# A state-space layer with a dense network on one core: K permuted and transposed by DMA, table G loaded without its zeros

## The chip, the core and the metric

The kernel runs on one core of a Trainium2 chip. A core has a matrix engine (PE; its weight loads are listed apart as PEld), a vector engine (DVE), a scalar engine (ACT), a general engine (POOL) and a queue engine (SP) that issues most transfers. Each takes its own instructions strictly in order. The metric is the time of one execution in microseconds (us). Before the change the median of 3 runs is 222.39 us (221.74 to 222.77).

## What is computed

```python
x = A_q                                               # 2048 x 640, bf16
k_shift = sum over t of k_pad[:, t:t+S] * shift_k[:, 3-t]   # 4 taps along the sequence
kv = k_shift * v
y  = causal long convolution of kv with ssm_k (by FFT), bf16
y  = y + kv * ssm_D
h  = x + layernorm(x) * y
h2 = h + Mish(layernorm(h) @ w1 + b1) @ w2            # 640 -> 1728 -> 640
```

S is 2048 and D is 640, batch 1. All inputs and the output are bf16.

## The kernel before

The sequence position is split as 16 times t1 plus t2: a partition holds t1 (128), and 16 rows t2 lie in it. Channels are taken in five blocks m of 128. The long convolution is a Fourier transform in two steps, a product, and the inverse in two steps, all as matmuls with tables.

The steps, by the names that the order list uses (pe is the matmul, ev the copy of its result out of PSUM to SBUF):

- k1 (L635): transposes of the long filter ssm_k; s1k (L561, L562) its first transform step, s2k (L662) its second, with table G as weights. Results lie in tile uk. One s2k unit is three matmuls of 160 columns and one copy of 480 columns; s2k needs all copies of s1k.
- kt (L590): per block m, 16 matmul transposes of K into kt_s; ktev copies them out of PSUM (1024 bf16 columns at a time, 10 copies); ktsh (L601, POOL) writes a third plane, shifted by one position.
- wsh (L516, POOL): weights for the 4-tap filter from the coefficients (coef, computed by cfpe from shift_k) and a 16-wide mask.
- kspe (L609, L610): the 4-tap filter as matmuls of kt_s with wsh; kv (L613, DVE) multiplies by V while leaving PSUM.
- s1v (L561, L562) and s2v (L697): the two transform steps of kv, with G as weights; results in uv.
- sw (L678, L679, SP): copies uk with even and odd partitions swapped; p1 and p2 (L716, L720; DVE or POOL): the products.
- i1 (L756, L757) and i2 (L813): the inverse steps; y copies the result out of PSUM.
- ln1, lnx, wb, h, bn, hc: the two layer norms; trd (L849) transposes the normalized rows by DMA, trpe by matmul for the first two.
- m1 (L910, L890) with Mish on ACT (L915), m2 (L943, L931), res (L948), d_out.

ORDER, a list written into the kernel, gives each step its engine (t PE, v DVE, a ACT, p POOL, d SP's queue, s ACT's queue) and its place on that engine. `unit` makes a pair of matmul and copy, as halves x and y. Copies out of PSUM are done by ACT (L428) or DVE (L430). PSUM has 8 banks, handed out by the same order.

Channels are read as `(d m l)`, so that a block m takes every fifth group of four channels, and 128 elements of K (8 positions by 16 channels) lie at one step of 40. G is 128 blocks of 128 x 128, 32 KB a partition, and three quarters of it are zeros: a row for channel offset dl (row modulo 4) has values only in columns of the same offset.

SP's queue loads, in this order: ssm_k blocks 0, 2, 3; x (four tiles); ssm_k 1, 4; K in four parts; G in eight parts of 512 KB with V in two parts among them; then the swaps.

## Time and profile before

| | |
|---|---|
| median of 3 runs | 222.39 us |
| span of the profiled execution (first to last instruction) | 219.6 us |
| granted PE clock | 1.00 throughout |
| PE busy | 212.6 us |
| DVE busy | 145.1 us |
| ACT busy | 133.1 us |
| POOL busy | 75.6 us |
| moved by DMA | 31.03 MB |

The span of the profiled execution is 2.8 us below the median of the runs; the time around the span (start and end of the program) is in the runs only. In the rows of the profile L561 is line 561 of the kernel, `out<-in` names the tiles, and "idle before, releaser" says how long the engine waited ahead of such instructions and what ended the wait. Rows of the chain that ended last show start, duration, and the work; rows in order of time show start, duration, engine, line and count.

### The profile page before, as it was taken

To read this page: it belongs to the slowest core of one execution; us is meant where nothing else is said; L and a number is where in the kernel's file an instruction comes from. 1 tells how busy PE (TensorE), PEld (TensorE's weight loads), DVE (VectorE), ACT (ScalarE), POOL (GpSimd) and SP (SyncE) were. 2 spreads that over 40 slices of the span, in tenths; PEclk is the share of its full clock that TensorE was granted. 3 is DMA by queue.
4 is the path that set the end of the run, shared out by engine and by line. 5 is a ranking of instruction groups with operands and counts; after the bars stand their busy time and mean duration, and the time that the engine had idled before them with its cause. 6 is when DMAs were issued, how large, how long until landed. Compare 5 with 4: busy or idle time off the path is not lost.

```text
span 219.6 us, 6285 instructions
## 1 busy us (share of the span) xinstructions
PE 212.6 (97%) x2611; PEld 157.8 (72%) x2618; DVE 145.1 (66%) x324; ACT 133.1 (61%) x265; POOL 75.6 (34%) x112
## 2 busy tenths in 40 slices
PE   8999999999989999999999999999999999999993
PEld 2899889999879999899876644566554444656672
DVE  0799999999999999989699889883210000213023
ACT  2488899999999999997881178600036475300000
POOL 0079997089844007124883371411000000000000
PEclk9999999999999999999999999999999999999999
DMA  6999993417999906996004401552720000000113
GB/s 213 375 419 414 412 403 130 98 23 174 192 263 285 380 10 217 325 359 105 0 0 64 91 14 45 50 103 60 86 79 19 0 3 0 0 0 3 54 60 125
DMA packets 32876, 31.03 MB, mean 141 GB/s; under 512 B 19024, under 2 KB 29264, under 8 KB 32464
## 3 DMA queue, kind: packets, MB, share of 16 engines
q1 hardware_dynamic: 32384, 30.43, 46.3%
q8 instruction: 20, 0.33, 0.7%
q10 hardware_dynamic: 368, 0.20, 0.4%
q14 instruction: 8, 0.07, 0.1%
q0 software_dynamic: 96, 0.00, 0.0%
HBM read 20.47 MB, written 2.62 MB: 105 GB/s over the span
## 4 chain that ended last, share of the span: by engine, by line
PE 76%; ACT 11%; DVE 5%; issue 3%; SPq 2%; DMA 1%; DVEq 0%; ACTq 0%
PE ps L943 26%; PE ps L910 26%; ACT uk L428 8%; PE ps L813 4%; ACT uv L428 3%; PE ps L756 3%; PE ps L757 3%; PE ps L635 2%; PE ps L561 2%; PE ps L473 2%; PE ps L590 2%; DMA xa<-uk 1%; DVE ra L613 1%; PE ps L931 1%; DVE uv L716 1%
## 5 line engine op out<-in xcount | busy, mean ns | idle before, releaser
L910 PE MATMUL ps<-G 128*128 128x512 bf16 (+1 forms) x319 | 58.5, 336 | 0.3
L943 PE MATMUL ps<-rn,uv 128*128 128x320 bf16 (+2 forms) x415 | 58.5, 299 | 0.1
L915 ACT ACTIVATE uv<-ps,b1s 128x512 bf16<-128x512 f32 (+1 forms) x65 | 35.6, 607 | 36.6 <-PE ps L910 34.8
L943 PEld LDWEIGHTS <-uv 128*128 128x128 bf16 x416 | 39.2, 98 | 18.5 <-issue 1.6
L910 PEld LDWEIGHTS <-G 128*128 128x128 bf16 x325 | 31.1, 98 | 24.0 <-issue 0.9
L428 ACT CAST uk<-ps 128x512 bf16<-128x512 f32 (+1 forms) x91 | 47.2, 703 | 1.9 <-PE ps L562 1.4
L948 DVE TENSOR_TENSOR xb<-ps,xb 128x320 bf16<-128x320 f32 (+2 forms) x12 | 5.6, 488 | 42.6 <-ACT uv L915 24.3
L428 ACT CAST uv<-ps 128x512 bf16<-128x512 f32 (+2 forms) x54 | 28.6, 766 | 0.0
L430 DVE CAST uk<-ps 128x512 bf16<-128x512 f32 (+2 forms) x32 | 20.1, 661 | 0.6 <-ACT uk L428 0.5
L756 PE MATMUL ps<-a,uv 128*128 128x128 bf16 x160 | 18.7, 219 | 0.4 <-DVE uv L716 0.3
L756 PEld LDWEIGHTS <-uv 128*128 128x128 bf16 x160 | 17.8, 114 | 0.9 <-DVE uv L716 0.5
L837 POOL TENSOR_TENSOR r<-ve,mhalf 128x1 f32<-128x1 f32 x16 | 9.7, 613 | 25.0 <-DVE ve L834 24.9
L430 DVE CAST uv<-ps 128x512 bf16<-128x512 f32 (+2 forms) x28 | 17.2, 669 | 0.2 <-ACT uv L428 0.2
L948 DVE TENSOR_TENSOR xa<-ps,xa 128x320 bf16<-128x320 f32 x12 | 5.6, 486 | 14.0 <-PE ps L943 13.9
L613 DVE TENSOR_TENSOR ra<-ps,rb 128x512 bf16<-128x512 f32 x20 | 12.9, 683 | 0.3 <-ACT uv L428 0.3
L720 POOL TENSOR_TENSOR rn<-rn,uv 128x1024 bf16<-128x1024 bf16 x5 | 10.6, 2127 | 7.2 <-PE ps L697 7.2
L697 PE MATMUL ps<-uv,G 128*128 128x64 bf16 (+1 forms) x256 | 12.2, 197 | 0.8 <-ACT uv L428 0.6
L662 PE MATMUL ps<-uk,G 128*128 128x160 bf16 x128 | 12.4, 230 | 0.3 <-ACT uk L428 0.2
L697 PEld LDWEIGHTS <-G 128*128 128x128 bf16 x256 | 10.8, 96 | 1.4 <-issue 1.0
L428 ACT CAST rb<-ps 128x512 bf16<-128x512 f32 (+1 forms) x30 | 11.3, 464 | 0.7 <-PE ps L813 0.4
L561 PE MATMUL ps<-cst,ra 128*64 128x128 bf16 x160 | 10.7, 219 | 0.4
L562 PE MATMUL ps<-cst,ra 128*64 128x128 bf16 x160 | 10.9, 222 | 0.0
(111 smaller groups left out, 375.7 us busy)
## 6 DMA issues: line engine op xcount, KB each, us to landing
G<-tab_g SPq DMA_DIRECT2D x8, 512.0 KB, 14.1
rn<-in_A_ssm_k_dram SPq DMA_DIRECT2D x5, 512.0 KB, 6.3
ra<-in_A_k_dram SPq DMA_DIRECT2D x4, 640.0 KB, 11.4
rb<-in_A_v_dram SPq DMA_DIRECT2D x2, 1280.0 KB, 13.9
G<-in_B_w_dram SPq DMA_DIRECT2D x5, 432.0 KB, 7.3
rn<-in_B_w_dram SPq DMA_DIRECT2D x1, 2080.0 KB, 13.4
rn<-uk SPq DMA_DIRECT2D x8, 256.0 KB, 4.3
rb<-uk SPq DMA_DIRECT2D x8, 256.0 KB, 4.5
```

The costliest lines, as they stand in the source:

```text
L428: nc.scalar.copy(o, i)
L430: nc.vector.tensor_copy(o, i)
L561: nc.tensor.matmul(ps[0:64, k, :], lhs, mc, start=True, stop=True)
L562: nc.tensor.matmul(ps[64:128, k, :], lhs, ms, start=True, stop=True)
L613: nc.vector.tensor_tensor(kv_w[:, m, k:32:2, 8 * h:8 * h + 8, :], ps.rearrange("p (l t d) -> p d t l", l=4, t=8), raw_v[:, 8 * h:8 * h + 8 ...
L662: nc.tensor.matmul(ps[:, o:o + 160], g_v[:, f, :], KA[:, :, f, :], start=True, stop=True)
L697: nc.tensor.matmul(ps[:, fl * n:fl * n + n], g_v[:, f0 + h * kf + fl, :], VX[x][:, :, f0 + h * kf + fl, :], start=True, stop=True)
L756: nc.tensor.matmul(pz[:, k, :], V[c.i][:, dg // 4, :, dg % 4], a12[:, 0, :], start=True, stop=False)
L910: nc.tensor.matmul(ph[:, 0:w], w1[:, dc, fc * P:fc * P + P], lnhT_of(u)[:, dc, 0:w], start=(dc == 0), stop=(dc == NDC - 1))
L915: nc.scalar.activation(hb_of(u)[:, fc, 0:w], rt.tile[:, 0:w], ACT.Mish, bias=b1s[:, fc:fc + 1], scale=1.0)
L943: nc.tensor.matmul(po[:, 0:d1 - d0], hb_of(u)[:, fc, tl * P:(tl + 1) * P], w2[:, fc, d0:d1], start=False, stop=(fc == NFC - 2))
L948: nc.vector.tensor_tensor(x, rt.tile[:, 0:d1 - d0], x, ALU.add)
```

## The change

Channels are now read as `(m p)`, contiguous blocks of 128. K is no longer transposed by PE: a copy kp (10 of 1024 columns; POOL nine, ACT one) permutes it within SBUF into buffers KP, and a DMA transpose kx on SP's queue writes kt_s, whose planes now lie in one row of 272 so that the shifted plane is a slice of it. ktpe, ktev and ktsh are gone.

```diff
-                nc.tensor.transpose(ps[:, q, :], raw_k[:, h * 8 * D + r:(h + 1) * 8 * D:40], ident)
...
-            ev(e, kt_s[b][:, :, h, :], ps.bitcast(BF16).rearrange("p (q t) -> p q t", q=8))
...
-            nc.gpsimd.tensor_copy(t[:, :, 2, 1:128], t[:, :, 1, 0:127])
...
+                src = raw_k[:, h * 8 * D:(h + 1) * 8 * D].rearrange("p (t c) -> p t c", t=8)[:, :, m * P:(m + 1) * P].rearrange("p t (q j) -> p q t j", j=16)
+                out = KP[m, h].rearrange("p (q t j) -> p q t j", q=8, t=8)
+                if e == "act":
+                    nc.scalar.copy(out, src)
+                else:
+                    (nc.vector if e == "dve" else nc.gpsimd).tensor_copy(out, src)
+            kps[m, h] = OP(f"kp{m}_{h}", [("pool", 1.3), ("dve", 0.55), ("act", 0.95)], d_k[2 * h:2 * h + 2], emit=kpf)
+
+            def kxf(e, m=m, h=h):
+                nc.sync.dma_start_transpose(kt_s[m][:, :, 144 - 128 * h:272 - 128 * h], KP[m, h])
+            kxs[m, h] = OP(f"kx{m}_{h}", ("dma", 1.5), [kps[m, h]], emit=kxf, lat=2.6)
```

KP lies in xb, in the hc tile and in the part of rn that held ssm_k blocks 2 to 4, so kp4_1 and the five kp of h = 0 wait for the k1 transposes of those blocks, and the swaps into rn wait for the kx.

```diff
+    KP = {(m, 1): x for m, x in enumerate([xb[:, 0:1024], xb[:, 1024:2048], xb[:, 2048:3072], hc_t[:, 0:1024], rn[:, 2 * S:2 * S + 1024]])}
+    KP |= {(m, 0): rn[:, 2 * S + 1024 * (m + 1):2 * S + 1024 * (m + 2)] for m in range(NDC)}
...
+    for i, k in enumerate([(4, 1)] + [(m, 0) for m in range(NDC)]):
+        kps[k].deps += k1_by[2 + i // 2]
```

G is stored without its zeros (1 MB) and loaded by eight transfers of 32 partitions by 16 pieces of 256 bytes; four memsets of 4096 columns (gz) write zeros first, one on DVE and three on POOL. Within a group of four blocks the columns are interleaved, so that a weight load now reads with a step of four elements. Each half of G needs four of the loads, and s2k and s2v wait for a half.

```diff
-    g_v = gt[:].rearrange("p (f q) -> p f q", q=P)
+    g_v = gt[:].rearrange("p (b q f) -> p b f q", q=P, f=4)
...
-        return lambda: nc.sync.dma_start(gt[:, i * 2048:(i + 1) * 2048], dram["g"][:, i * 2048:(i + 1) * 2048])
+        d, h = i % 4, i // 4
+        return lambda: nc.sync.dma_start(gt[d:P:4, h * 8192:h * 8192 + 8192].rearrange("p (b q) -> p b q", q=512)[:, :, 128 * d:128 * d + 128], dram["g"][d, :, h * 2048:h * 2048 + 2048].rearrange("p (b q) -> p b q", q=128))
+    c_gz = [OP(f"gz{i}", [("dve", 2.2), ("pool", 4.2)], emit=(lambda e, i=i: (nc.vector if e == "dve" else nc.gpsimd).memset(gt[:, i * 4096:(i + 1) * 4096], 0.0))) for i in range(4)]
...
-    d_g = [DMA(f"d_g{i}", 0.525e6, emit_g(i), deps=d_n[:1], prio=0.6, lat=4.9) for i in range(8)]
+    d_g = [DMA(f"d_g{i}", 0.131e6, emit_g(i), deps=d_n[:1] + c_gz[i // 4 * 2:i // 4 * 2 + 2], prio=0.6, lat=3.5) for i in range(8)]
```

Smaller edits follow from the new channel order: shift_k is loaded in pieces of 4 elements (8 bytes), ssm_D by five rows and one matmul instead of four, the coefficients are written four times over (1760 columns instead of 440), the mask has 176 columns, kv and y write contiguous runs.

```diff
-    d_sk = OP("d_sk", ("dmaS", 0.5), [d_row1], emit=lambda e: nc.scalar.dma_start(sk_r[:], A_shift_k.rearrange("(d n) j -> d (n j)", n=40)), lat=5.0)
+    d_sk = OP("d_sk", ("dmaS", 0.5), [d_row1], emit=lambda e: nc.scalar.dma_start(sk_r[:].rearrange("p (n j) -> p n j", j=4), A_shift_k.rearrange("(n d) j -> d n j", d=16)), lat=5.0)
...
-        ev(e, coef[:], cf_rt.tile[:, 0:440])
+        ev(e, coef[:].rearrange("p (r l) -> p r l", l=4), cf_rt.tile[:, 0:440].unsqueeze(2).to_broadcast([P, 440, 4]))
```

ORDER is written anew. Up to the first i2 matmul ACT has 4 k1, 26 s1k, 29 s2k, 28 s1v, 32 s2v and 33 i1 copies and one kp (before 3, 25, 32, 24, 30, 33 and 4 ktev); DVE has 6 k1, 14 s1k, 14 s2k, 12 s1v, 10 s2v, 5 i1 copies, 20 kv, 30 products and one memset (before 7, 15, 11, 16, 12, 4, 20, 27 and 6 ktev). Of the lnx 9 run on POOL instead of 7, and ACT has 29 y copies instead of 30. PE does all of s1k ahead of s2k, and 26 s2k units ahead of the first kspe. The new orders of POOL and of SP's queue:

```
POOL: gz1 gz3 kz gz0 wsh1_1 wsh1_0 wsh0_0 kp1_0 kp0_0 kp4_0 ln1p1 wsh0_1 kp0_1 kp2_1 kp1_1 kp2_0 wsh4_0 wsh2_0 kp3_1 wsh3_0 kp4_1 wsh3_1 wsh2_1 wsh4_1 p2_0_1 p2_0_3 d_small p1_0_0 p1_0_2 ...
SP:   d_n0 d_n2 d_x0 d_n1 d_n3 d_n4 d_g6 d_g7 d_k1 d_g5 d_k0 d_g4 d_g2 d_k3 d_k2 d_g1 d_g0 d_g3 d_v1 kx0_0 d_v0 kx0_1 kx1_0 kx1_1 kx3_0 kx2_0 kx2_1 kx3_1 kx4_0 kx4_1 sw0_0 sw0_1 sw0_3 sw0_2 sw1_0 sw2_1 ...
ACT:  warm k1ev0y k1ev2y s1kev0_2x s1kev0_1x s1kev2_3y s1kev0_2y s1kev0_3y s1kev2_2x coef ... kp3_0 (after the last s1kev) s2kev_20y ...
```

## The prediction

> **What bounds the kernel now.** I read the busy time by stretches first, because shares over the whole span mix stages. The columns are the stretch, its length, then busy time of PE, PEld, DVE, ACT and POOL, the granted clock, the DMA share and GB/s.

> ```profile
> core 0: us, PE busy (x) PEld busy (x) DVE busy (x) ACT busy (x) POOL busy (x), PEclk, DMA share, GB/s
> 0.00:8.30 8.30, 7.32 (x51) 3.92 (x53) 2.01 (x8) 1.49 (x2) 0.52 (x10) 1.00 0.79 261
> 8.30:34.00 25.70, 25.14 (x552) 23.56 (x553) 24.69 (x50) 23.06 (x41) 21.23 (x24) 1.00 1.02 410
> 34.00:87.00 53.00, 51.20 (x1093) 48.36 (x1092) 52.09 (x86) 53.00 (x112) 26.27 (x24) 1.00 0.62 169
> 87.00:96.00 9.00, 9.00 (x97) 7.84 (x95) 8.70 (x23) 8.78 (x24) 1.74 (x3) 1.00 0.97 344
> 96.00:216.00 120.00, 119.63 (x828) 73.98 (x834) 57.23 (x161) 46.77 (x89) 25.88 (x53) 1.00 0.24 49
> ```

> The last row is the dense network (m1, m2): PE works 119.63 of 120 us, and the change takes nothing from its matmuls. Whatever the change is worth, it is by how much earlier that block starts. Ahead of it, from 34 to 87 us, ACT has no idle time at all and DVE 0.9 us: the copies out of PSUM set the pace. PE looks as busy, but a busy PE in this view is not a full one.

> The waits of ACT up to 90 us are the next view (who waited for whom: total, times, longest), then two rows in order of time that show where each of the two engines starts.

> ```profile
> ACT rb L428 <- PE ps L635: 5.2, 1, 5.2
> ACT uk L428 <- PE ps L562: 1.4, 2, 0.7
> ACT uv L428 <- PE ps L590: 0.7, 1, 0.7
> ACT uk L428 <- PE ps L662: 0.5, 1, 0.5
> 6.73 0.69 DVE L430 COPY xa<-ps 128x1024 bf16<-128x1024 bf16 x1 [0.28 <-PE ps L635]
> 8.31 1.01 ACT L428 COPY rb<-ps 128x1024 bf16<-128x1024 bf16 x1 [5.20 <-PE ps L635]
> ```

> ACT begins copying at 8.31 us, 1.6 us after DVE, and later waits for PE for 1.4 + 0.7 + 0.5 = 2.6 us, before 34 us, while PE also transposes K (L590). After that it never waits. So the front can end sooner in two ways: less copying for ACT and DVE together, or a better filled beginning.

> **The change part by part.** The ledger of the two copying engines, from groups kept apart by shape (busy us, then mean ns; I divide busy by count, since the means overlap):

> ```profile
> L428 ACT CAST uk<-ps 128x512 bf16<-128x512 f32 x59 | 30.0, 710 | 1.4 <-PE ps L562 1.4
> L428 ACT CAST uv<-ps 128x512 bf16<-128x512 f32 x35 | 19.9, 795 | 0.0
> L428 ACT CAST uk<-ps 128x480 bf16<-128x480 f32 x32 | 17.3, 692 | 0.5 <-PE ps L662 0.5
> L428 ACT COPY uv<-ps 128x1024 bf16<-128x1024 bf16 x4 | 4.0, 1030 | 0.7 <-PE ps L590 0.7
> L428 ACT CAST coef<-ps 128x440 bf16<-128x440 f32 x1 | 0.5, 532 | 0.0
> L430 DVE CAST uk<-ps 128x512 bf16<-128x512 f32 x21 | 13.5, 675 | 0.6 <-ACT uk L428 0.5
> L430 DVE COPY uv<-ps 128x1024 bf16<-128x1024 bf16 x6 | 3.9, 680 | 0.0
> L716 DVE TENSOR_TENSOR uv<-uv,uk 128x1024 bf16<-128x1024 bf16 x12 | 8.1, 700 | 0.0
> ```

> ACT, by the new order up to the first i2 matmul: four K copies go (-4.0); one more k1 copy (+1.0, the 1024 row), one more s1k (+0.5), four more s1v and two more s2v0 (6 x 0.57 = +3.4), three fewer s2k (-3 x 0.54 = -1.6), kp3_0, a copy of 1024 elements (+1.0). The coefficient copy grows from 440 to 1760 columns; from 512 to 1024 columns an ACT copy rises by 0.49 us, so 1320 more are +1.3. Sum: +1.6 us.

> DVE: six K copies go (-3.9); s1k, s1v, s2v0, s2k, i1 and k1 by count -1 -4 -2 +3 +1 -1, at 0.64 each -2.6; three more products p1/p2 (3 x 0.68 = +2.0). Sum -4.5 us. The memset of a quarter of G (gz2, 2048 words as it is built) falls into DVE's idle first six microseconds and costs nothing; without that hole it would be about 1.7 us by the rate of the row below (64 words 0.11 us, nearly all of it proportional at worst).

> Together the two lose 2.9 us of work, 1.45 us each if shared evenly, but the order gives ACT more, not less. What pays for it is the start: k1ev0y, ready when DVE took its copy at 6.73 us, is now ACT's first copy beside DVE's k1ev0x, so ACT starts 1.6 us earlier; and the 80 transposes on PE, behind which ACT waited, are gone.

> ```profile
> 18.42 4.60 PE ps L590 x72
> 30.03 0.38 PE ps L662 x3
> 41.63 0.31 PE ps L697 x8
> L697 PEld LDWEIGHTS <-G 128*128 128x128 bf16 x256 | 10.8, 96 | 1.4 <-issue 1.0 <-DVE uv L430 0.2
> L756 PEld LDWEIGHTS <-uv 128*128 128x128 bf16 x160 | 17.8, 114 | 0.9 <-DVE uv L716 0.5 <-issue 0.3
> 76.32 0.06 PE ps L757
> 95.94 3.87 PE ps L910 x35
> ```

> 72 transposes took 4.60 us, so 80 give PE 5.1 us back. Against it, G is now read as weights with a step of four elements. L756 already reads weights so: 114 ns instead of 96, a matmul every 0.06 us. The 160-column matmuls (0.38 us for 3) hide that. The 64-column ones come every 39 ns (0.31 for 8): if each must wait for 57 ns, 128 of them cost 2.3 us, the 96-column ones less than that again. Bounds 0 and 4.6 us of PE; I take 2. PE stays 3 us lighter and, by ACT's waits, is not the bound after 34 us, so this is nothing on the path, and 2 us if PE were.
> [...]

> **Transfers.** Rows: the loads at full rate, the swap of 256-byte pieces, the landing of G's loads and of the transposes (median us), and one transpose's time on SP's queue.

> ```profile
> 10.00:22.00 12.00, 11.93 (x254) 11.39 (x249) 11.70 (x28) 10.52 (x19) 9.51 (x12) 1.00 1.02 417
> 37.00:41.00 4.00, 3.92 (x113) 3.69 (x108) 4.00 (x8) 4.00 (x10) 0.57 (x2) 1.00 0.66 133
> G<-tab_g SPq DMA_DIRECT2D x8, 512.0 KB, 14.1
> G<-hc SPq DMA_TRANSPOSE x14, 2.7
> 121.94 1.21 SPq L849 DMA_TRANSPOSE G<-hc  x1
> ```

> G falls from 4.2 MB (10 us at 417 GB/s) to 1.05 MB in 256-byte pieces. Between 37 and 41 us one swap of such pieces ran at 133/0.66 = 200 GB/s, so about 5.2 us. Up to the last G load the queues now carry 3.3 MB (ssm_k, x), 2.6 MB (K) and G: 7.9 + 6.3 + 5.2 = 19.4 us, so G is complete near 22 to 24 us. s2k starts when ACT has done 26 s1k copies, four k1 and the coefficients: 6.7 + 13.2 + 4 + 1.8 = 25.7 us (30.0 before). G is in time with 2 us to spare; K, interleaved with it, too.

> The ten kx transposes are 1024 columns where trd has 640: 1.6 times 1.21 = 1.94 us each on SP, landing 1.6 x 2.7 = 4.3 us after issue. The bounds are 1.21 (the size doesn't matter) and 4.3 (each waits until the one before it has landed). Queued behind them on SP: v0 and then the swaps.

> ```profile
> L516 POOL TENSOR_TENSOR uv<-cst,coef 128x704 bf16<-128x704 bf16 x5 | 6.8, 1366 | 0.8 <-ACT coef L428 0.8
> L601 POOL COPY uv<-uv 128x1016 bf16<-128x1016 bf16 x5 | 5.1, 1029 | 0.0
> L716 POOL TENSOR_TENSOR uv<-uv,uk 128x1024 bf16<-128x1024 bf16 x4 | 8.5, 2126 | 0.2
> L467 DVE MEMSET hc<- 128x64 uint32 x1 | 0.1, 112 | 0.8 <-PEq L980 0.8
> ```

> POOL loses five shifts (-5.1) and three products (-6.4), and gets nine kp copies: 1.03 each by the plain copy, 2.13 by the dearest POOL operation of that size; they are plain copies, so I take 1.1. Each of its three memsets lies between 2.1 (2048 words at the copy's rate) and 4.1 us (4096 elements); I take 3. POOL is through the memsets at 10 (13) us, ahead of the coefficients at 13.6. Then in its order: three wsh 17.7, three kp 21.0, ln1p1 22.1, wsh0_1 23.5, kp0_1 24.6. kx0_1 lands at 24.6 + 4.3 = 28.9. The first kspe stands behind 26 units of s2k, one per 0.29 us (0.58 on two engines): 25.7 + 7.5 = 33.2. The last, kx4_1, is issued after eight more, 24.6 + 8 x 1.94 = 40.1, and lands at 44.4; kspe4 stands at about 49 (41 s2k, 20 s1v and s2v, 12 kv). So the chain is hidden by some 4.5 us at both ends, with kp at 2.13 by almost nothing.
> [...]

> The weights table wsh, kv and y keep their counts and sizes; only steps change: no cost either way that a row shows. The shift coefficients now arrive in 8-byte pieces ahead of cfpe on PE; ACT has copies queued until about 12 us, so a delay of a microsecond or two is covered.

> **Sum.** Along ACT: -1.6 (start), -2.6 (waits on PE) and +1.6 (ledger) = -2.6 us if no new wait appears; if half of the old waits come back in another place, -1.3. I take -2.0. The profiled span of 219.6 becomes 217.6. The runs' median is 2.8 us above that span (222.39), so 220.4.

> **Rivals.**
> (a) The K chain is late. The deciding point: kx4_1 must land by 49, so (49 - 4.3 - 24.6)/8 = 2.5 us a transpose on SP; my 1.94 is scaled from one on a quiet queue. Midway to the upper bound, at 3.1 us, it lands at 24.6 + 24.8 + 4.3 = 53.7, and with kp at 2.13 us (four copies ahead of kx0_1) 4 us later still, so 5 to 9 us late; I price it at 6. kspe is in PE's order, so all later s1v and s2v wait, and the swaps behind it on SP too: 220.4 + 6 = 226.4. For it: no copies are left over that could fill the hole. Against it: DMA share between 34 and 87 us was only 0.62 and drops with G gone.
> (b) Nothing measurable. ACT is the front's bound and gets 1.6 us more; if its waits at the start merely move (G in full before s2k, the coefficients), the two gains shrink to 1.6: 222.4.
> (c) All three engines were jointly full: PE's 5.1 us and the 2.9 us of copies both show, -4.5: 217.9. It is 5.1 - 2 = 3.1 of PE and 1.45 of copies. For it: PE's row is 51.2 of 53. Against: ACT's own ledger rises.
> (d) The sparse load doesn't do what it says: read from memory the pieces run at half the swap's rate, 10.4 us for G; with 2 us of slack s2k, which needs four loads for each half, starts 3.2 us late: 223.6. Against it: the queues would then carry as long as before, and before s2k began at 30 us with G still loading.

> **How the numbers follow.** Forecast (219.1 to 221.2) 0.34, (c) 0.14, (b) 0.16, (a) 0.24, (d) 0.12. A difference under 0.5% (1.1 us) is about what a measurement of this kernel can't tell from none. Faster 0.48, same 0.16, slower 0.36. The range has to reach (c) and (a): 217.3 to 226.4; the forecast's own is 219.1 to 221.2.

> **What would show it.** Right: ACT's first copy near 6.7 us, no row of ACT waiting for PE over 1 us before 34 us, the first s2k matmul near 26 us, the first long m1 stretch (L910 in the row above) at 94 instead of 95.94 us. (a): PE waiting on a transpose ahead of kspe, ACT and DVE idle around 30 to 55 us. (d): PE waiting for G at 22 to 28 us. (c): ACT's front busy time falls. I am wrong in the ledger if ACT is idle for more than 2 us between 26 and 85 us, or if the m1/m2 stretch is no longer PE without gaps.

## The result, and the profile after

The changed kernel takes 227.62 us (median of 4 runs, 227.2 to 227.78), the kernel before beside it 222.45 us: a ratio of 1.0248 (95% interval 1.0214 to 1.0281), 5.2 us slower. The profiled execution of the changed kernel has a span of 225.4 us where the kernel before has 219.6. The prediction was 220.4 us.

The busy time by stretches of the changed kernel, in the columns of the prediction's first view, with the bounds moved to its own stages:

```profile
core 0: us, PE busy (x) PEld busy (x) DVE busy (x) ACT busy (x) POOL busy (x), PEclk, DMA share, GB/s
0.00:8.30 8.30, 7.32 (x44) 3.96 (x44) 3.07 (x7) 2.78 (x4) 7.77 (x13) 1.00 0.80 275
8.30:34.00 25.70, 20.56 (x439) 18.98 (x438) 19.64 (x41) 21.41 (x39) 18.76 (x17) 0.93 1.13 310
34.00:55.00 21.00, 20.16 (x473) 19.20 (x470) 19.79 (x34) 20.48 (x43) 10.54 (x8) 1.00 1.05 175
55.00:93.00 38.00, 33.74 (x663) 31.35 (x661) 36.36 (x55) 35.23 (x74) 22.06 (x27) 1.00 0.86 279
...
101.70:222.00 120.30, 119.97 (x832) 73.51 (x830) 57.87 (x163) 44.31 (x87) 27.74 (x55) 1.00 0.17 39
```

The dense network is as long as before (120.3 us against 120) and as full; it starts at 101.6 instead of 95.9 us, which is the difference of the two profiled spans (5.8 us; the medians differ by 5.2). Between 8.3 and 34 us, where PE had 0.6 us of idle time, it now has 5.1, and ACT 4.3 (2.6 before). From 55 to 93 us PE, DVE and ACT all have holes (4.3, 1.6 and 2.8 us). From 8.3 to 34 us the DMA share is 1.13 at 310 GB/s where it was 1.02 at 410: the queues are as full as before, with fewer bytes.

The waits of PE up to 102 us, then ACT's first copies, in order of time:

```profile
PE ps L502 <- DMA sk_r<-in_A_shift_k_dram: 3.0, 1, 3.0
PE ps L659 <- ACT uk L429: 1.4, 1, 1.4
PE ps L753 <- DVE uv L713: 1.4, 1, 1.4
...
PE ps L694 <- ACT uv L429: 0.8, 1, 0.8
PE ps L753 <- ACT uk L429: 0.8, 1, 0.8
PE ps L606 <- DMA uv<-xb: 0.7, 1, 0.7
```

```profile
7.01 1.01 ACT L429 COPY xa<-ps 128x1024 bf16<-128x1024 bf16 x1 [3.69 <-PE ps L630]
8.02 1.01 ACT L429 COPY rb<-ps 128x1024 bf16<-128x1024 bf16 x1
8.93 3.16 ACT L429 CAST uk<-ps 128x512 bf16<-128x512 f32 x6
14.31 1.62 ACT L429 CAST coef<-ps 128x1760 bf16<-128x1760 f32 x1 [2.23 <-PE ps L502]
17.96 1.07 ACT L429 CAST uk<-ps 128x512 bf16<-128x512 f32 x2 [2.02 <-PE ps L563]
```

ACT starts at 7.01 us, as forecast, and then stands for 2.2 + 2.0 us because PE waits 3.0 us for the coefficients (L502). Only one row of PE's names a K transpose (L606, 0.7 us, at 39.7 us, after kspe has begun), so by this view alone the K chain would look harmless. The next view, SP's queue in order of time, shows why it is not:

```profile
20.24 0.62 SPq L534 DMA_DIRECT2D rb<-in_A_v_dram  x1
22.28 1.92 SPq L597 DMA_TRANSPOSE uv<-rn  x1
24.39 0.89 SPq L534 DMA_DIRECT2D rb<-in_A_v_dram  x1
29.05 1.24 SPq L597 DMA_TRANSPOSE uv<-xb  x1
30.38 3.37 SPq L597 DMA_TRANSPOSE uv<-rn  x1
33.84 1.26 SPq L597 DMA_TRANSPOSE uv<-xb  x1
35.20 3.90 SPq L597 DMA_TRANSPOSE uv<-rn  x2
```

The transpose kx0_1, forecast to have landed by 28.9 us, is issued at 29.05. A transpose holds SP for between 1.24 and 3.4 us here; what sets it these rows don't show. Three rows of POOL's show why kx0_1 goes so late, and one of PE's what it meets:

```profile
16.02 4.28 POOL L515 TENSOR_TENSOR uv<-cst,coef 128x704 bf16<-128x704 bf16 x3 [4.66 <-ACT coef L429]
24.25 1.03 POOL L593 COPY rn<-ra 128x1024 bf16<-128x1024 bf16 x1 [2.00 <-PE ps L630]
27.98 3.00 POOL L593 COPY xb<-ra 128x1024 bf16<-128x1024 bf16 x3
29.85 5.95 PE L659 MATMUL ps<-uk,G 128*128 128x160 bf16 x77 [1.41 <-ACT uk L429]
```

POOL's first wsh starts at 16.02 us and not at 13.6, because the coefficients are late, and a K copy waits 2.0 us for the transposes of ssm_k (L630). So kp0_1, the first copy of the third row, ends at 29.0 us where 24.6 was forecast. kx0_1 then lands at 34.9 us. Nobody waits for it in this kernel: PE works on s2k, itself 4.2 us later than forecast, from 29.85 to 35.8 us and starts kspe right behind it. The two late inputs cover each other, with 0.9 us between them.

All kernels that ran, with where the stages lie in the trace (us from the span's start: the first s2k matmul, the first and last matmul of the K filter kspe, the first i1 matmul):

| kernel | median us | ratio to before, 95% interval | s2k from | kspe | i1 from |
|---|---|---|---|---|---|
| before | 222.45 | 1 | 30.0 | 25.3 to 49.8 | 66.7 |
| after | 227.62 | 1.0248 (1.0214 to 1.0281) | 29.9 | 35.8 to 54.9 | 72.1 |
| e1_sk_on_sp | 228.11 | 1.0297 (1.0264 to 1.0331) | 25.7 | 35.5 to 56.3 | 72.9 |
| e2_coef_late | 226.85 | 1.0249 (1.021 to 1.0288) | 27.4 | 36.7 to 57.3 | 73.5 |
| e3_before_sk8 | 222.88 | 1.0046 (1.0011 to 1.0081) | 30.4 | 25.6 to 50.2 | 67.1 |
| e4_v_first | 227.13 | 1.0255 (1.0202 to 1.0308) | 25.6 | 35.0 to 54.6 | 71.5 |
| e5_kx_plain | 224.84 | 1.0123 (1.0086 to 1.0161) | 25.9 | 33.2 to 51.5 | 68.6 |
| e6_kx_plain_v_first | 224.26 | 1.01 (1.0059 to 1.0141) | 26.4 | 33.2 to 51.4 | 68.7 |
| e7_before_gsparse | 222.51 | 1.0026 (1.0008 to 1.0043) | 30.9 | 25.8 to 50.8 | 67.9 |
| e8_k0_first | 229.66 | 1.0301 (1.0258 to 1.0344) | 26.6 | 32.5 to 56.5 | 74.5 |
| e9_g_whole | 232.22 | 1.0461 (1.0421 to 1.0501) | 32.0 | 40.4 to 58.7 | 76.5 |
| e10_act_first | 222.14 | 0.9996 (0.9977 to 1.0014) | 29.8 | 25.0 to 49.6 | 66.5 |
| e11_v_on_act | 229.63 | 1.0332 (1.0301 to 1.0362) | 30.1 | 38.4 to 56.6 | 73.8 |
| e12_k0_first_v_on_act | 231.22 | 1.0423 (1.0375 to 1.047) | 31.2 | 39.4 to 57.7 | 76.2 |
| e13_v_on_act_after_g | 230.7 | 1.0381 (1.0305 to 1.0457) | 31.6 | 39.8 to 58.1 | 76.4 |
| e14_v_on_act_behind_kp3 | 230.12 | 1.0357 (1.0323 to 1.0392) | 25.9 | 37.7 to 57.4 | 74.6 |
| e15_v_on_pool | 228.94 | 1.0331 (1.0294 to 1.0368) | 26.3 | 36.1 to 56.0 | 73.1 |

In every row i1 starts 16 to 18.5 us behind the last kspe (16.9 before, 17.2 after), and the dense network starts about 29 us after i1. The time goes with the end of the K filter; an earlier s2k alone moves nothing (after and e1). The stages of e2 are those of its slowest execution, 228.56 us. The dependencies offer a reason, which no run tests by itself: the swaps of chunks 1 and 2 write over V's tile and so wait for the last kv, and the last of s1v and s2v stand behind it on PE and the copying engines.

### The profile page after: what moved, and what is told of

It reads as the page before. It is cut to its first block, busy times and chain, and to the rows that moved or that the text cites. A ratio compares the mean times of both kernels' runs of the same rounds, so it can differ in the third digit from the quotient of the medians.

```text
span 225.4 us, 6149 instructions
## 1 busy us (share of the span) xinstructions
PE 211.0 (94%) x2535; PEld 155.1 (69%) x2535; DVE 145.7 (65%) x319; ACT 132.6 (59%) x263; POOL 88.1 (39%) x120
## 4 chain that ended last, share of the span: by engine, by line
PE 76%; DMA 11%; ACT 6%; DVE 3%; SPq 1%; issue 1%; ACTq 0%; DVEq 0%
PE ps L940 25%; PE ps L907 24%; DMA sk_r<-in_A_shift_k_dram 4%; ACT uk L429 4%; PE ps L753 4%; PE ps L754 4%; PE ps L810 4%; PE ps L562 3%; DMA uv<-xb 3%; PE ps L694 2%; DMA G<-hc 2%; PE ps L630 2%; DMA rb<-uk 2%; PE ps L605 2%; DVE uk L431 1%; PE ps L928 1%
## 5 line engine op out<-in xcount | busy, mean ns | idle before, releaser
L907 PEld LDWEIGHTS <-G 128*128 128x128 bf16 x325 | 31.0, 98 | 24.8 <-issue 1.7
L429 ACT CAST uk<-ps 128x512 bf16<-128x512 f32 (+1 forms) x88 | 44.4, 684 | 4.6 <-PE ps L754 2.1
L429 ACT CAST uv<-ps 128x512 bf16<-128x512 f32 (+2 forms) x60 | 30.0, 634 | 0.8 <-PE ps L563 0.7
L431 DVE CAST uk<-ps 128x512 bf16<-128x512 f32 (+2 forms) x35 | 21.4, 659 | 1.5 <-PE ps L659 0.8
L834 POOL TENSOR_TENSOR r<-ve,mhalf 128x1 f32<-128x1 f32 x16 | 10.5, 663 | 29.7 <-DVE ve L831 29.7
L753 PEld LDWEIGHTS <-uv 128*128 128x128 bf16 x160 | 17.8, 113 | 2.4 <-DVE uv L713 2.4
L515 POOL TENSOR_TENSOR uv<-cst,coef 128x704 bf16<-128x704 bf16 x10 | 14.3, 1454 | 4.7 <-ACT coef L429 4.7
L431 DVE CAST uv<-ps 128x512 bf16<-128x512 f32 (+2 forms) x22 | 13.5, 663 | 0.2 <-PE ps L694 0.2
L609 DVE TENSOR_TENSOR ra<-ps,rb 128x512 bf16<-128x512 f32 x20 | 12.8, 683 | 0.9 <-PE ps L606 0.7
L713 DVE TENSOR_TENSOR uv<-uv,uk 128x1024 bf16<-128x1024 bf16 (+1 forms) x15 | 11.8, 809 | 1.5 <-POOL rn L717 1.4
L659 PE MATMUL ps<-uk,G 128*128 128x160 bf16 x128 | 11.2, 232 | 1.5 <-ACT uk L429 1.4
L562 PE MATMUL ps<-cst,ra 128*64 128x128 bf16 x160 | 11.3, 219 | 1.0 <-DVE uv L431 0.6
L429 ACT CAST rb<-ps 128x128 bf16<-128x128 f32 (+1 forms) x29 | 11.0, 469 | 1.7 <-PE ps L810 1.7
## 6 DMA issues: line engine op xcount, KB each, us to landing
rn<-in_A_ssm_k_dram SPq DMA_DIRECT2D x5, 512.0 KB, 7.6
```

What stands on the lines that cost most here:

```text
L429: nc.scalar.copy(o, i)
L431: nc.vector.tensor_copy(o, i)
L515: (nc.gpsimd if e == "pool" else nc.vector).tensor_tensor(out, a, b, ALU.mult)
L562: nc.tensor.matmul(ps[0:64, k, :], lhs, mc, start=True, stop=True)
L609: nc.vector.tensor_tensor(kv_w[:, m, 16 * k:16 * k + 16, 8 * h:8 * h + 8, :], ps.rearrange("p (d t l) -> p d t l", t=8, l=4), raw_v[:, 8 * ...
L659: nc.tensor.matmul(ps[:, o:o + 160], g_v[:, f // 4, f % 4, :], KA[:, :, f, :], start=True, stop=True)
```

## The experiments

### Is it the late coefficients? (e1, e2, e3)

The coefficients (sk_r) landed 10.0 us after issue instead of 4.4. Three kernels deal with them: the load moved to SP's queue behind ssm_k block 2; its use moved further back on PE and ACT; and, in the kernel before, the load alone changed to 8-byte pieces (there the coefficients are then in another order, and the output with them).

```diff
# e1, on the changed kernel
-    d_sk = OP("d_sk", ("dmaS", 0.5), [d_row1], emit=lambda e: nc.scalar.dma_start(...
+    d_sk = OP("d_sk", ("dma", 0.5), [], emit=lambda e: nc.sync.dma_start(...
-ORDER: d_n0:d d_sk:s warm:a d_n2:d
+ORDER: d_n0:d warm:a d_n2:d d_sk:d
# e2, on the changed kernel
+ORDER: cfpe:t behind s1kpe2_0x:t, coef:a behind s1kev2_0x:a
# e3, on the kernel before
-    nc.scalar.dma_start(sk_r[:], A_shift_k.rearrange("(d n) j -> d (n j)", n=40))
+    nc.scalar.dma_start(sk_r[:].rearrange("p (n j) -> p n j", j=4), A_shift_k.rearrange("(n d) j -> d n j", d=16))
```

> The changed kernel, with the transfer of the 8-byte pieces of shift_k moved from ACT's queue, where its packets alternate with the big loads, onto SP's queue behind the second block of ssm_k. Theory A (the late shift coefficients are the main loss: PE stood 3.0 us at the coefficient matmul, and started again at a granted clock of 0.79 to 0.87): shift_k lands by about 7 us, PE has no wait there, and the time falls by 4 to 5 us, to 222.5 to 223.5. Rival B (K's chain through POOL and the transposes is the main loss): the time gained at the start is lost again at the first filter matmul, and the time falls by less than 1.5 us, to 226 or more. Rival C (copies: more ACT work than before sets the front): between these, about 225.

> The changed kernel, with the coefficient matmul placed seven units later on PE and the coefficient copy two copies later on ACT; transfers as they are. Theory A: PE fills the wait with transposes of ssm_k and s1k, POOL gets the coefficients no earlier than before; 3 to 4.5 us less than the changed kernel, 223 to 224.6. Rival B: under 1.5 us less.

> The kernel before, with one edit: shift_k is loaded in 8-byte pieces, as in the changed kernel (in its channel order, so the coefficients are those of other channels and the output is another). Theory A: the transfer lands near 11 to 13 us instead of 6, PE waits some 2 to 3 us at the coefficient matmul and loses clock; 2 to 4.5 us more than before, 224.5 to 227. Rival B: the wait is covered by copies, under 1 us more, up to 223.4.

In e1 the coefficients landed 5.7 us after issue, no wait for them is left, and s2k starts at 25.7 us, the very time of the prediction. The time did not fall (228.11 us): rival B holds. The waits of PE up to 60 us in e1, and three stretches of it:

```profile
PE ps L605 <- DMA uv<-xb: 4.1, 1, 4.1
PE ps L659 <- DVE uk L431: 1.2, 1, 1.2
```

```profile
30.00:35.00 5.00, 1.46 (x20) 1.26 (x17) 2.33 (x4) 3.35 (x8) 5.00 (x6) 0.97 1.31 204
35.00:40.00 5.00, 4.47 (x49) 4.48 (x50) 2.00 (x4) 1.02 (x2) 4.18 (x3) 0.50 1.33 193
40.00:45.00 5.00, 5.00 (x111) 4.93 (x111) 4.23 (x7) 4.62 (x10) 0.00 (x0) 0.85 1.30 172
```

What is saved at the front is spent ahead of kspe: PE waits 4.1 us, until 35.5, for kx0_1, the transpose that kspe reads first, which is issued at 25.85 us and lands 9.6 us later. PE's clock is at half from 34.7 to 41.5 us, and ACT does 1.02 us of work in the five microseconds from 35. So the late coefficients are real (3.0 us of PE) but cover another lateness of the same size; e2, whose ratio (1.0249) is that of the changed kernel, says the same. In the kernel before, where the 8-byte load lands 7.1 us after issue, it costs 0.5% (0.1 to 0.8%).

### Is it the transposes, or V's place? (e4, e5, e6)

All three stand on e1. e4 issues V's two loads together, ahead of kx0_0. e5 replaces the ten transposes by plain copies of as many bytes between the same tiles, in 256-byte pieces (the filter then reads untransposed K, so the output is another). e6 does both.

```diff
# e4 and e6
-ORDER: d_v1:d ... kx0_0:d ... d_v0:d kp0_1:p kx0_1:d
+ORDER: d_v1:d d_v0:d ... kx0_0:d ... kp0_1:p kx0_1:d
# e5 and e6
-    nc.sync.dma_start_transpose(kt_s[m][:, :, 144 - 128 * h:272 - 128 * h], KP[m, h])
+    nc.sync.dma_start(kt_s[m][:, :, 144 - 128 * h:272 - 128 * h], KP[m, h].rearrange("p (q t) -> p q t", q=8))
```

> As e1 (shift_k on SP's queue), and V's second half goes onto SP's queue ahead of the first transpose instead of between the first and the second. In e1 the second transpose was issued at 25.9 us and PE waited 4.3 us for it, to 35.5 us, and ran at half clock for 6.8 us after that. Theory B1 (the transpose is late because it stands behind V in one queue and the two kinds of transfer do not overlap): the second transpose lands near 32 us, PE waits under 2 us and keeps its clock; 3 to 5 us less than e1, 223 to 225. Rival B2 (the transposes themselves and POOL's copies are slow, wherever they stand): the first filter matmul stays at 35 us and the time within 1 us of e1.

> As e1, with each DMA transpose of K replaced by a plain copy of the same 256 KB between the same tiles in 256-byte pieces (K is not transposed, so the output is another). Theory B3 (it is the transposing that makes the queue slow: idle gaps before and after each one): the copies run at the swaps' 200 GB/s, 1.3 us each, without gaps; the second lands near 31 us, no long wait of PE; 4 to 6 us less than e1, 222 to 224. Rival B1 (place in the queue): V still stands between the first two copies; under 2 us less than e1.

> Both edits of e4 and e5 (output another). If the K chain is the whole loss of the changed kernel, its front is free here and the forecast's sum holds: 220 to 222. If this is above 224, the loss lies behind the K chain, in the swaps and products.

e4 took 227.13 us and e1 228.11, which the intervals of their ratios don't tell apart. Nor does e4 test V's place for kx0_1, since V's second half stands ahead of that transpose in both; it still lands 8.9 us after issue, and kspe stays at 35.0 us, as rival B2 had it. Plain copies take off 3.3 us (228.11 to 224.84), clear of noise and between the ranges of B3 and B1. A plain copy in the place of kx0_1 still lands 7.6 us after issue, behind the same V. The edit changes three things together, the gaps in the queue, the time that SP is held (0.62 us for that copy, 2.43 for the transpose) and the records, and what each is worth stays open.

With plain copies the first kspe stands at 33.2 us. That this is the prediction's own time is in part chance, since PE still waits there, 1.6 us in e5 and 1.1 us in e6. e6 is above the 224 that its expectation set as the limit: what is left to the kernel before, 2.2 us (1.3 to 3.1), is there with little lateness. kspe comes 8 us later in PE's order than before (33.2 against 25.3) and ends 1.6 us later.

The trace of single transfers shows what goes on in SP's queue. For each microsecond, the records started: those of 256 bytes are K's transposes or copies (1024 records each), those of 10240 bytes are V.

```
us     changed kernel          e5, plain copies
       256 B     10240 B       256 B     10240 B
25         0        40            15        33
26       466         8           701        13
27        27         3           247        33
28       531        16            61        36
29         0        45            17        41
30         0        33           729         9
31        77        32           812         4
32       429         1           574         0
33       220         1           755         0
34      1120         0           796         0
```

In this queue the transfers go nearly one behind the other: most of kx0_1's records go when V's second half is through. Transposes alone ran at 1120 records in a microsecond (changed kernel, at 34 us), so one needs an estimated 0.9 us. But between V's records and a transpose's there are microseconds with next to nothing (27 us: 30 records), which the plain copies do not have.

### The other parts of the change (e7, e9, e10)

e7 gives the kernel before the sparse load of G with its memsets and the step-four weights. e9 gives the changed kernel the whole table, in the new column order, and no memsets. e10 exchanges one copy in the kernel before, so that ACT starts as early as in the changed one.

```diff
# e7, on the kernel before: G's eight loads and four gz as in the change
+    return lambda: nc.sync.dma_start(gt[d:P:4, ...][:, :, 128 * d:128 * d + 128], ...)
+    c_gz = [...]
# e9, on the changed kernel
+    return lambda: nc.sync.dma_start(gt[:, i * 2048:(i + 1) * 2048], dram["g"][:, i * 2048:(i + 1) * 2048])
-ORDER: gz0:p gz1:p gz3:p gz2:v
# e10, on the kernel before
-ORDER: k1ev0y:v ... k1ev2x:a
+ORDER: k1ev0y:a ... k1ev2x:v
```

> The kernel before with the sparse load of G alone (its table, four memsets, step-four weights, waits by halves). Forecast's ledger: the big loads end near 26 us instead of 33, but ACT and DVE set the pace, and nothing comes of it: 221 to 223. If the step-four weights cost PE 2 us on the path: 224. If the loads bound the start of before: 219 to 221.

> The changed kernel with table G loaded whole (4.2 MB instead of 1.05) and no memsets; all else as changed. Theory A (the sparse load is what leaves the queues room for K): G and K together need 7.6 us more of the queues, the last K piece and the last piece of G land near 30 us instead of 22, the K filter starts 4 to 7 us later than at 35.8 us and the time is 230 to 234 us. Rival C (the memsets and the 256-byte pieces cost as much as they save, or the wait for the transposes hides the load): 226.5 to 228.5 us, as the changed kernel.

> The kernel before, with one copy exchanged: ACT takes k1ev0y, the first that is ready, and DVE takes k1ev2x in its place. By the term of the prediction (ACT's start 1.6 us earlier is worth up to 1.6 us): ACT's first copy at about 6.8 us instead of 8.31 and 220.8 to 221.5 us, ratio 0.993 to 0.996. Rival D (the end of the K filter sets the time, and PE, not the copies, sets that end): ACT starts earlier but the filter ends at 49.8 us as before and the time is the same to 0.3 us.

e7: 222.51 us, 0.26% over before: the sparse load gains nothing there, and what it may save less what memsets and step-four weights cost is at most 1 us of loss (1.0043 at the upper end). e9: 232.22 us. The filter starts 4.6 us later than in the changed kernel, as theory A had it; so the sparse load is what this K chain lives on. (The coefficients too landed 1.0 us later in e9, and PE waited 1.5 us longer for them, which may be a part of it.) Two stretches of e9, with the queues at full rate until 30 us:

```profile
20.00:25.00 5.00, 4.85 (x136) 4.27 (x130) 4.97 (x10) 4.97 (x10) 3.66 (x4) 1.00 1.02 410
25.00:30.00 5.00, 3.94 (x103) 3.35 (x99) 4.97 (x11) 4.86 (x10) 3.46 (x6) 1.00 1.04 420
```

e10, ACT in order of time:

```profile
6.60 1.01 ACT L428 COPY xa<-ps 128x1024 bf16<-128x1024 bf16 x1 [3.48 <-PE ps L635]
8.70 2.72 ACT L428 CAST uk<-ps 128x512 bf16<-128x512 f32 x5 [1.08 <-PE ps L562]
```

ACT starts 1.7 us earlier than before, and the time is the same (ratio 0.9996, 0.9977 to 1.0014, so worth at most 0.5 us). A wait of 1.08 us comes back at once, and the filter ends at 49.6 us. Rival D's numbers came in: an earlier start of ACT is worth next to nothing here. That PE is what sets the filter's end is not shown by them.

### Can the K transposes be had in time? (e8, e11 to e15)

e8 (on e4) makes kp0_0 and kp0_1 first on POOL and issues kx0_0 and kx0_1 ahead of V. e11 is e4, and e12 is e8, with V issued from ACT's queue; in e13 V stands behind kp3_0 in the list, in e14 it waits for kp3_0; e15 is e8 with V on POOL's queue.

```diff
# e8
+ORDER: d_g3:d wsh0_0:p kp0_0:p kp0_1:p kx0_0:d kx0_1:d d_v1:d d_v0:d wsh0_1:p kp1_0:p kp1_1:p wsh1_1:p wsh1_0:p
# e11 to e14 (e15: nc.gpsimd, engine "pool", d_v1:p d_v0:p behind kp0_1:p)
-    d_v = [DMA(f"d_v{h}", 1.31e6, emit_v(h), ...
+    d_v = [OP(f"d_v{h}", ("dmaS", 0.7), [], emit=lambda e, h=h: emit_v(h)(), lat=8.0) for h in range(2)]
-    nc.sync.dma_start(rb[:, h * half:(h + 1) * half], ...
+    nc.scalar.dma_start(rb[:, h * half:(h + 1) * half], ...
# e13 and e14
+ORDER: kp3_0:a d_v1:s d_v0:s
# e14
+    for o in d_v:
+        o.deps.append(kps[3, 0])
```

> Theory A (the transposes serialise with other transfers on SP's queue; the first two stand behind V and behind POOL work that they don't need): with the coefficients on SP's queue, kp0_0 and kp0_1 made right after the first weights (wsh0_0) and kx0_0, kx0_1 issued ahead of V, the first K transposes land by about 27 us, PE's wait ahead of kspe (3.8 to 4.3 us in the two kernels before) falls under 1 us, the K filter ends near 52 instead of 56 and the time is about 224.5 us (223.5 to 225.5). Rival B (all ten transposes and V share one queue, so who goes first only moves the wait): the first wait goes, but V or kx1 come later, PE waits there instead, the filter still ends at 54.5 or later and the time stays at 226.5 to 228 us.

> The kernel with the coefficients on SP's queue and V ahead of the transposes (227.1 us), V's two loads now issued from ACT's queue. Theory A (transposes and plain loads hold each other up because they stand in one queue): kx0_0 and kx0_1 take 1.3 us each of SP instead of 4.3 and 5.1, PE's wait ahead of kspe (3.8 us) falls under 1 us, the K filter ends near 52 and the time is about 224.5 us. Theory E (a transpose and a plain load hold each other up wherever they stand, since both need the same sixteen DMA engines): kx0_0 and kx0_1 still take over 3 us together with V's landing, the wait stays between 2.5 and 4.5 us, and the time is 226.5 to 227.5 us.

> The kernel with K's first two transposes ahead of V (229.7 us), V's two loads now issued from ACT's queue. Theory A (one queue): the first K transposes land by 28 us and V by 32, no wait over 1 us is left on PE between 26 and 45 us, the filter ends near 51.5 as with plain copies, about 224.3 us. Theory E (one set of DMA engines): the transposes kx1 and later still take 4 to 5 us each while V lands, the filter ends after 54, 227 to 229.5 us.

> As the kernel with K's first two transposes first and V on ACT's queue (231.2 us), but V is issued from ACT behind kp3_0, at about 27 us, when G has landed, so that V is in flight beside the transposes alone. Theory A (they hold each other up because they stand in one queue): kx1_0 and those behind it take about 1.3 us each of SP while V lands (four in 5.3 us), V lands within 9 us, the filter ends by 53 and the time is 224 to 226 us. Theory E (one set of DMA engines, whatever the queue): with V in flight between 27 and 36 us a transpose takes 3 us or more of SP, as in the kernel with V on SP behind the first two (5.15 and 4.30), and the time is 227 to 230 us.

> As the run before was meant: V from ACT's queue, now made to wait for kp3_0, so that it is issued at about 27 to 28 us, after G has landed and beside the K transposes alone. (In the run before it still went at 21.25 us, beside G.) Theory A (one queue): kx1_0 and those behind it take about 1.3 us each of SP while V lands, V lands within 9 us, the filter ends by 53 and the time is 224 to 226 us. Theory E (one set of DMA engines, whatever the queue): with V in flight a transpose takes 3 us or more of SP and the time is 227 to 231 us.

> As the kernel with K's first two transposes first (229.7 us, V on SP behind them), but V's two loads come from POOL's queue, issued behind kp0_1 at about 25 us. POOL's transfers count on semaphores of their own, so no issue on SP waits for V's landing, as the issues did in the runs with V on ACT's queue (8.6 to 8.8 us). Theory A (the transposes lose time because they stand in one queue with plain loads): kx0_1, kx1_0 and kx1_1 take 1.3 us each of SP while V lands, the filter ends by 53 and the time is 224 to 226 us. Theory E (they share DMA engines and slow each other down whatever the queue): with V in flight from 26 to 35 us a transpose takes 2.5 us or more of SP, the first pair lands after 32 us, and the time is 227 to 230 us.

SP's queue in e1, where V's second half stands ahead of kx0_1, and then in e8, where V stands behind it (`xb` is kx0_1's source):

```profile
24.20 1.02 SPq L534 DMA_DIRECT2D rb<-in_A_v_dram  x1
25.85 2.43 SPq L597 DMA_TRANSPOSE uv<-xb  x1
```

```profile
25.07 1.99 SPq L597 DMA_TRANSPOSE uv<-xb  x1
27.12 1.09 SPq L534 DMA_DIRECT2D rb<-in_A_v_dram  x2
28.30 5.15 SPq L597 DMA_TRANSPOSE uv<-rn  x1
```

In e8 the first wait is gone: kx0_1 lands 3.3 us after issue, at 28.4 us, where it took 9.6 us in e1, and kspe starts at 32.5, ahead of the 33.2 of the forecast. This pair shows that V ahead in the queue made the transpose late. But other waits come: the product kv (L609, DVE) waits 2.1 us for POOL's copies, since it writes over the K that they read, and 1.3 us for V, which is now late; PE waits for DVE, 1.4 us for kx1_0 and 0.8 us for kx1_1. The filter ends at 56.5 us, and the time, 229.66, is above the ranges of both theories. Rival B holds in its mechanism: who goes first only moves the wait.

e11 to e14 took 229.63, 231.22, 230.7 and 230.12 us (ratios 1.0332, 1.0423, 1.0381 and 1.0357). The first three are above the ranges of both theories, the fourth lies in theory E's, and they answer another question than the one put. The waits of SP's queue in e11, then in e14:

```profile
SPq L541 <- DMA rb<-in_A_v_dram: 8.8, 1, 8.8
SPq L675 <- DMA uv<-rn: 1.9, 1, 1.9
```

```profile
SPq L597 <- DMA rb<-in_A_v_dram: 8.6, 1, 8.6
SPq L541 <- DMA ra<-in_A_k_dram: 2.9, 2, 1.6
```

SP stands 8.8 us ahead of a load of G, and in e14 8.6 us ahead of kx0_1, until V has landed, though neither reads V. In the trace of the changed kernel the transfers of SP and ACT count on eight semaphores in turn (100, 102, 104, 105, 106, 108, 109, 110), and an issue that comes to one again first waits on it: there a load of G waited 2.1 us for the coefficients, which came by ACT's queue on 109 and landed at 13.13 us, and was issued at 13.15. By these waits V on ACT's queue held the one that G's load (8.8 us in e11, 8.6 in e12; in e13 three loads of G take 10.49 us of SP's queue) or kx0_1 (e14) came to next. So none of the four put V beside the transposes alone for more than about a microsecond, and e14's time is in theory E's range for another reason than the theory's. In e13 V's second half was moreover issued at 21.25 us, much as in e12 (20.81), because the list is sorted by planned start. In e11 to e13 V's first half goes from ACT at 3.1 us already, beside ssm_k, which is a further difference to e4 and e8.

e15 does put V beside the transposes: POOL's transfers have other semaphores (111 to 113 in the kernel before and in the changed one), and none of SP's waits from 14 to 50 us in e15 is for V. SP's queue in e15, in order of time:

```profile
24.92 2.03 SPq L597 DMA_TRANSPOSE uv<-xb  x1
28.67 3.34 SPq L597 DMA_TRANSPOSE uv<-rn  x1
32.10 3.75 SPq L597 DMA_TRANSPOSE uv<-xb  x1
...
39.65 1.32 SPq L597 DMA_TRANSPOSE uv<-xb  x1
41.07 1.30 SPq L597 DMA_TRANSPOSE uv<-hc  x1
```

The records started in each microsecond of e15, transposes on SP's queue against V on POOL's:

```
us                     27   28   29   30   31   32   33
256 B (transposes)     32   35   45   50   46   33  183
10240 B (V)            26   36   44   35   45   31   21
```

While V is in flight, from 27 to 33 us, the two queues start about as many records each (32 to 50 against 26 to 45 in a microsecond), so the transposes' 256-byte records get about a fortieth of V's bytes: some 40 records in a microsecond where the changed kernel had 1120 at 34 us. Transposes hold SP for 2.0 to 3.75 us and for 1.3 us when V is through; the filter runs from 36.1 to 56.0 us, the time is 228.94. kx0_1 lands 11.2 us after issue, and only this first transpose holds SP for less than the 2.5 us of theory E, whose range the time is in: another queue did not help. That the shared DMA engines are the reason is the theory's argument; the counts fit it.

## Why the prediction was wrong, step by step

**The first step that failed** is "kx0_1 lands at 24.6 + 4.3 = 28.9", with its conclusion that the chain "is hidden by some 4.5 us at both ends". In e1, where the coefficients come in time, POOL is 1.2 us later than the sum has it (issue at 25.85), but the landing takes 9.6 us where the sum has 4.3, a size scaled from trd on a quiet queue. The sum had no term for what stands ahead of the transpose in SP's queue. "Queued behind them on SP: v0 and then the swaps" misreads the change's own order, in which d_v0 stands ahead of kx0_1 and of the eight transposes after it. At the 410 GB/s of the other loads V's 2.6 MB are an estimated 6.4 us. With V behind it (e8) the same transpose lands after 3.3 us. In the changed kernel itself the issue, at 29.05, is late by POOL's waits, and the whole is hidden behind a late s2k, so that taking the late coefficients away alone gains nothing (e1).

**The coefficients** were said to be "covered" for "a microsecond or two". They landed at 13.1 instead of 6.1 us (10.0 us after issue instead of 4.4, and issued 1.4 us later); PE waited 3.0 us and ACT 2.2 + 2.0. The cover was mis-sized, but the term is worth nothing by itself here, since e1 takes it away without gain.

**The second step that failed** is the path of the sum, "Along ACT: -1.6 (start), -2.6 (waits on PE) and +1.6 (ledger)", of which it says "I take -2.0". "so ACT starts 1.6 us earlier" came true to 0.3 us (7.01 against 6.7) and is worth at most 0.5 us (e10). The 2.6 us of waits on PE were gone as well in e1, and came back as 5.9 us behind 34 us, ahead of kspe (ACT's waits in e1). The prediction read "After that it never waits" as a bound set by ACT's work, but the time goes with the end of the K filter. e6 shows it without the first step's failure: it meets the forecast's own schedule within 0.7 us, with s2k from 26.4, kspe from 33.2 and the last four of the filter's twenty units, kspe4 "at about 49" among them, from 48.8. It is still 2.2 us slower than the kernel before, where the forecast had 2.0 us faster. In the kernel before the last four units start at 45.8 us and the filter ends at 49.8, against 51.4 in e6; the prediction set its own filter beside its transposes, and never beside the filter of before.

Of the 7.2 us between forecast and result some 3.9 are this path (220.4 to e6's 224.26), and some 3.4 the late inputs and the transposes themselves (224.26 to 227.62). Why the new order ends the filter later is argued, not tested: PE does all of s1k and 26 units of s2k first, so that the filter starts 8 us later than before and is then done in less time, 18 us instead of 24.5.

**What held.** kp 1.04 us (1.1 taken); wsh 1.45 (1.37 taken); POOL through the memsets at 11.4 us; kx0_1's landing with V behind it 3.3 us (e8; 4.3 taken). The shortest holds of SP by a transpose, 1.24 to 1.32 us, are at the lower bound given, not the 1.94 taken, but with other transfers in flight there are holds of up to 5.15 us (e8). G's last piece landed at 25.3 us (22 to 24 forecast), in time for s2k in the changed kernel and by about half a microsecond in e1; rival (d) has no row for it. The step-four weights took 115 ns a load (96 before), and e7 shows no net cost of them beyond 1 us. The records of the transposes alone ran at 1120 x 256 bytes in a microsecond, 287 GB/s (changed kernel, at 34 us). The memsets were 3.5 us each on POOL (3 taken) and 1.77 on DVE. These are the rows:

```profile
L515 POOL TENSOR_TENSOR uv<-cst,coef 128x704 bf16<-128x704 bf16 x10 | 14.3, 1454 | 4.7 <-ACT coef L429 4.7
L542 POOL MEMSET G<- 128x4096 bf16 x3 | 10.5, 3511 | 0.3 <-POOLq L977 0.3
L593 POOL COPY rn<-ra 128x1024 bf16<-128x1024 bf16 x5 | 5.1, 1041 | 2.0 <-PE ps L630 2.0
```

**Rival (a)** was right in its place, the K transposes, but not in its mechanism: it put the lateness at the last transposes and made it hang on 2.5 us a transpose. The late ones are the first, and the cause is the queue ahead of them, not their number. That its 226.4 is near the 227.62 measured is luck.

## What to carry to other kernels

kx0_1 landed 9.6 us after issue with V's second half ahead of it in its queue (e1), and 3.3 us after issue with V behind it (e8): add up the bytes that are issued ahead of a transfer in its queue, and do this for small and urgent transfers first. Two late inputs can hide each other: a wait in the profile that is removed without gain (3.0 us for the coefficients) says that the next one stands right behind it (4.1 us for kx0_1 in e1). Find which stage's end the later stages follow (here the K filter, 16 to 18.5 us ahead of i1 in every kernel run), and set its end in the new order against its end in the old one, before counting work off an engine that only looks full.
